# Three edits to an attention-plus-MLP kernel on one Trainium2 core: states of the last output pieces, the rule ahead of each logits step, and the first w1 loads

## The chip, the core and the metric

The kernel runs on one core of a Trainium2 chip. The core has five engines with instruction streams of their own: TensorE (PE, matmuls and their weight loads), VectorE (DVE), ScalarE (ACT), GpSimd (POOL) and SyncE (SP), which here issues all DMAs. They meet at semaphores. Matmul results go to PSUM, which has eight banks of 512 float32 columns on 128 partitions. The metric is the device time of one execution in microseconds, as the median over several executions. Less is better.

## The reference

The inputs are x (2048 tokens by 1024), four 1024 x 1024 weights, a gate per head and an MLP over tokens with hidden size 3584. All are bfloat16. Cut to what matters:

```python
xn = layernorm(x)
# A: 32 heads of 32, 4 segments of 512 tokens, a memory M, z carried from segment to segment
q, k, v = heads(xn @ wq), heads(xn @ wk), heads(xn @ wv)
for s in range(4):
    p     = softmax(qs @ ks.T * scale + causal_mask)
    a_dot = p @ vs
    a_mem = (phi(qs) @ M) / (phi(qs) @ z + 1e-6)
    o_s   = g * a_mem + (1 - g) * a_dot
    M, z  = M + phi(ks).T @ vs, z + sum(phi(ks))
A = concat(o_s) @ wo
# B: token-mixing MLP, over tokens and not over features
h = layernorm(xn)
B = (gelu(h.T @ w1 + b1) @ w2 + b2).T
out = x + A + B
```

So one sum of three parts comes out, and the MLP mixes the 2048 tokens: w1 is 2048 x 3584 and w2 is 3584 x 2048.

## The kernel before

**Framework.** The program is straight-line. A `Res` is the state of a buffer: its last writer and its readers. `FW.op`, `FW.dma` and a matmul group call `_waits`, which makes the engine wait for the writer of what is read and, for what is written, for its writer and its readers:

```python
        for r in writes:
            ...
            for t in r.r.values():
                add(t)
```

A store to DRAM records itself as a reader of the buffer state that it is given. `FW` also keeps a planned clock of each engine (`now`, `clock`, `settle`), on which the order of the attention part is worked out while the program is built. All matmuls are issued in `mm`, so that the profile shows them on line 217; all DMAs are on line 245.

**Start (`loads`, `norm_and_first_hidden`).** x comes in 16 chunks of 128 tokens (256 KB each), and the first 512 columns of w1 in 16 chunks of 128 rows (128 KB each). SyncE issues them in a written-out order: x0, x1, w1 chunk 0, x2, x3, w1 chunks 1 to 3 in one, x4, x5, w1 chunks 4 and 5, and so on. For each chunk c: mean and variance (`stats`, on ScalarE for c in `ACT_STATS`, which has 1, 2, 4, 6 and so on, otherwise on VectorE), the factor 1/sigma (`scale`, GpSimd), the normalised h (`ln_h`, VectorE, line 837), and `early_hidden(c)`, which is eight matmuls of 512 columns on TensorE into all eight banks. VectorE's order is h of x0, h of x1, the statistics of x3, h of x2, half the statistics of x5, h of x3, and so on. Before any data is there, `warm` runs fourteen matmuls on zeros.

**Hidden (`hidden`).** The other 24 blocks of 128 hidden units, two halves each, sixteen matmuls a half, with gelu on ScalarE. TensorE is the bound there.

**Attention and output (`attention_and_out`).** Heads come in units of four; a pass p takes two units. A pass has these TensorE steps in a given list (`crit`): a logits step (`window(p, 0)`), q and k projections, a second logits step, a v projection, four weighing steps (`weigh`: p @ v, for later segments also the memory), a third logits step, q and k, four weighing steps, v. A logits step has ten or twelve matmuls with 32 rows each into six or seven banks at once; ScalarE takes the exponential of each bank (line 1073), which empties it, and GpSimd masks the diagonal blocks (line 1081). A logits step is a `wall`: no later step of the list is taken before it.

Between them go **dense steps** (`_Fill`): the second MLP product, one matmul of 512 columns each. A dense group makes half of one block of 128 output tokens: 28 steps for the 3584 hidden units, and for blocks of the first three segments eight more with wo. It holds one bank from its first step to its last, after which VectorE empties the bank into `stg` (line 1341). `left()` tells the steps that the open group still has:

```python
    def left(self):
        return 0 if self.at == 0 else self.size() - self.at
```

It gives 0 when no group is open. `can(now)` is true when the next dense step has its inputs and, for the first of a group, a free bank by the planned clock. `_Flow.run` picks, at each point of TensorE's planned clock, a step of the list if one is ready (its banks free for 120 ns, `MARGIN`) and the dense work is not behind its goal for this pass (`GOALS`), otherwise a dense step. The rule on line 505 holds back a logits step while an open group has one to five steps left.

**Tail (`tail`).** The last segment's output rows, which hold x and the MLP part already, are loaded back into `fin[0..3]`. For each of the eight pieces (i, h) of 128 rows by 512 columns, `part` adds the wo product in eight matmuls, VectorE adds the bank to `fin` (line 1253), and SyncE stores the piece. The first five pieces are taken in three rounds over the heads, since the last heads come late. The last piece (3, 1) is cut into columns 0 to 256 and 256 to 512, and both halves use the state `R_fin[3][1]`. At the very end SyncE waits for all stores (line 272).

Of the kernel before, what the change touches and what calls it, by code (L numbers as in the profile page):

```python
# [346 lines left out]
def _after(*groups):  # L347

    toks = {}
    for r in groups:  # L350
        for t in list(r.r.values()) + ([r.w] if r.w is not None else []):
            cur = toks.get(t.key)
            if cur is None or cur.val < t.val:
                toks[t.key] = t
    return toks
# [7 lines left out]
class _Flow:  # L363
# [118 lines left out]
    def run(self, goals):  # L482
        fw, fill = self.fw, self.fill
        stall = 0
        for t in self.crit:
            self.in_stage[t.stage] = self.in_stage.get(t.stage, 0) + 1
        self.stage_n = dict(self.in_stage)
        while self.crit:
            now = fw.now["pe"]
            nxt = self.advance(now)  # L490
            pick, soon = None, []
            for t in self.crit[:self.LOOK]:
                if t.left == 0 and len(self.free) >= t.banks:
                    bs = sorted(self.bank_t(b) for b in self.free)[:t.banks]
                    r = max([fw.ready(t.reads, t.writes)] + bs)
                    if r + self.MARGIN <= now:
                        pick = t
                        break
                    soon.append((r, t))
                if t.wall:  # L500
                    break
            stage = self.crit[0].stage
            n_left = self.in_stage[stage]
            ahead = fill.done >= goals[stage] + (goals[stage + 1] - goals[stage]) * (1 - n_left / self.stage_n[stage])
            if pick is not None and (ahead or not fill.can(now)) and not (pick.wall and 0 < fill.left() <= 5
                                                                          and fill.can(now)):
                self.emit_pe(pick)
                continue
            if fill.can(now):
                fill.step()  # L510
                continue
            late = [t for r, t in soon if r <= now]
            if late:
                self.emit_pe(late[0])
                continue
            when = [x for x in [r for r, _ in soon] + [nxt, fill.when()] if x is not None]
            when = [x for x in when if x > now] or [now + 50]
            fw.now["pe"] = min(when)
            stall += min(when) - now
            self.stalls.append((now, min(when) - now, [t.fn.__qualname__ for t in self.crit[:2]], fill.at))  # L520
        self.stall = stall
        return stall
# [21 lines left out]
class _Kernel:  # L544
# [170 lines left out]
    def loads(self):  # L715
        fw = self.fw
        fw.op("pool", lambda e: e.memset(self.mhalf[:], -0.5), writes=[self.R_mhalf])
        fw.op("pool", lambda e: e.memset(self.brow[:], 0.0), writes=[self.R_brow, self.R_brow2])
        fw.op("act", lambda e: e.activation(self.ln_t[:, 0, 0:1], self.mhalf[:, 0:1], ACT.Gelu_apprx_tanh),
              reads=[self.R_mhalf], writes=[self.R_st[0]], ns=1500)  # L720
        self.load_x(0, 1)
        self.load_x(1, 1)
        self.load_w1(0, 1)
        self.load_x(2, 1)
        self.load_x(3, 1)
        self.load_w1(1, 3)
        for c in range(4, 16, 2):
            if c == 4:
                self.load_x(4, 1)
                self.load_x(5, 1)  # L730
            else:
                self.load_x(c, 2)
            self.load_w1(c, 2)
            if c == 6:
                fw.dma(self.brow[0:N_FCH, :], self.B_b1.rearrange("(c q) -> c q", q=P), reads=[self.R_brow],
                       writes=[self.R_brow])
                fw.dma(self.brow[32:32 + N_TCH, :], self.B_b2.rearrange("(c q) -> c q", q=P), reads=[self.R_brow2],
                       writes=[self.R_brow2])
        fw.dma(self.beta_sb[:], self.A_beta.partition_broadcast(P), writes=[self.R_beta])
        self.w1_srcs = [self.B_w1[:, fp * 256:(fp + 1) * 256].rearrange("(c p) f -> p c f", p=P)  # L740
                        for fp in range(N_FCH // 2)]
        fw.dma(self.w1slot[2], self.w1_srcs[2], writes=[self.R_w1s[2]])
        self.w1_next = 3
# [482 lines left out]
    def tail(self):  # L1226
        fw, fl = self.fw, self.flow
        s = N_SEG - 1
        e = _Arena(self.nc, self.early_base, self.early_end)
        wait = _after(*self.R_wv)  # L1230
        fin = [e.take(f"fin{i}", [P, D_MODEL], BF16) for i in range(4)]
        R_fin = [[Res(f"fin{i}_{h}", wait) for h in range(2)] for i in range(4)]
        for i in range(4):
            fw.dma(fin[i][:], self.out_d[:, 4 * s + i, :], reads=[self.R_out[4 * s + i]], writes=R_fin[i],
                   record_reads=False)
        self.fill_left = self.fill.total - self.fill.done
        self.fill.rest()
        fl.advance(10 ** 9)
        order = [(i, h) for i in range(4) for h in range(2)]
        bank = {}  # L1240

        def part(ih, j0, j1, c0=0, c1=512):
            i, h = ih
            if j0 == 0:
                bank[ih, c0] = fl.take_bank()
            b = bank[ih, c0]
            with fw.group(reads=[self.R_wo] + self.R_oT[s % 2][j0:j1], writes=[self.R_bank[b]] if j0 == 0 or j1 == 8 else []):
                for jc in range(j0, j1):
                    fw.mm(self.ps[:, b, c0:c1], self.oT[s % 2][:, jc, i * P:(i + 1) * P],
                          self.wo_sb[:, jc, h * 512 + c0:h * 512 + c1], start=(jc == 0), stop=(jc == 7))  # L1250
            if j1 == 8:
                dst = fin[i][:, h * 512 + c0:h * 512 + c1]
                fw.op("dve", lambda e: e.tensor_tensor(dst, self.ps[:, b, c0:c1], dst, op=ALU.add),  # L1253
                      reads=[self.R_bank[b], R_fin[i][h]], writes=[R_fin[i][h]], ns=170 + (c1 - c0))
                fl.free.append(b)
                fw.dma(self.out_d[:, 4 * s + i, h * 512 + c0:h * 512 + c1], dst, reads=[R_fin[i][h]],
                       writes=[Res("o")], is_output=True)

        for j0, j1 in ((0, 6), (6, 7)):
            for ih in order[:5]:  # L1260
                part(ih, j0, j1)
        for ih in order[:5]:
            part(ih, 7, 8)
        for ih in order[5:7]:
            part(ih, 0, 8)
        part(order[7], 0, 8, 0, 256)
        part(order[7], 0, 8, 256, 512)


class _Fill:  # L1270
# [121 lines left out]
```

## Time and profile before

| what | value |
|---|---|
| median of 6 runs | 696.36 us (696.27 to 696.82) |
| the profiled execution | 696.82 us, of which the span of instructions is 694.8 us |
| TensorE busy | 688.5 us (99%), clock granted 1.000 |
| VectorE, ScalarE, GpSimd busy | 268.1, 282.0, 117.5 us |
| DMA | 77.32 MB, 111 GB/s mean over the span, 319 in the first fortieth |

By stage, with TensorE's busy time in each:

| stretch (us from the start) | what | TensorE busy |
|---|---|---|
| 0 to 9.24 | loads, first normalisations, warm-up, chunk 0 | 7.25 |
| 9.24 to 214.8 | first MLP product, first projections | 205.56 |
| 214.8 to 676.9 | attention passes with dense steps | 461.47 |
| 676.9 to 694.8 | tail | 14.21 |

Times in the trace count from the start of the span. Each instruction has its start, its length and, where its engine sat idle ahead of it, what ended that idle time (`<-`). A matmul of 512 columns is shown with 379 ns, but matmuls overlap: the next one starts 216 ns later. That spacing, and not the length, is what a matmul costs in a row of them.

### The profile page before, as it was taken

What the parts mean: (1) busy time and instruction counts of PE and PEld (TensorE: products, weight loads), DVE (VectorE), ACT (ScalarE), POOL (GpSimd) and SP (SyncE); (2) the same over time, 40 slices, a digit from 0 to 9 for tenths busy, and PEclk for the clock granted to TensorE, in tenths of its full rate; (3) what the DMA queues carried; (4) which work ended last, traced back from release to release, by engine and by line L of the source; (5) the groups of instructions that cost most, each with busy time, mean ns of one, the idle gap of its engine ahead of it and who ended that gap; (6) DMA issues with size and microseconds to landing.
All of it is one profiled execution on the core that took longest, in us unless ns stands there. A gap on an engine that the chain in (4) does not pass through costs nothing.

```text
span 694.8 us, 11585 instructions
## 1 busy us (share of the span) xinstructions
PE 688.5 (99%) x4822; PEld 329.2 (47%) x4822; DVE 268.1 (39%) x602; ACT 282.0 (41%) x513; POOL 117.5 (17%) x235
## 2 busy tenths in 40 slices
PE   8999999999999999999999999999999999999997
PEld 3444444444444544544445454444445444444553
DVE  6731100000002433434555464655546454444544
ACT  7431111122236364454544525454543525444350
POOL 5810000000001121221202212121212212121230
PEclk9999999999999999999999999999999999999999
DMA  9377666223038445446262543527263342524204
GB/s 319 107 182 180 153 169 202 84 60 101 1 122 169 103 94 133 105 105 137 46 153 65 124 102 75 124 52 152 49 150 83 85 109 53 121 62 107 50 18 142
DMA packets 211325, 77.32 MB, mean 111 GB/s; under 512 B 173770, under 2 KB 203594, under 8 KB 211274
## 3 DMA queue, kind: packets, MB, share of 16 engines
q1 hardware_dynamic: 211274, 76.59, 44.2%
q8 instruction: 38, 0.62, 0.4%
q14 instruction: 13, 0.11, 0.0%
HBM read 59.79 MB, written 5.24 MB: 94 GB/s over the span
## 4 chain that ended last, share of the span: by engine, by line
PE 97%; DMA 1%; SPq 0%; DVE 0%; ACT 0%; issue 0%; DVEq 0%
PE ps_all L217 97%; DMA w1all<-in_B_w_dram 1%; SPq L245 0%; DMA out_dram<-fin 0%; DVE fin L1253 0%; DVE stg L1341 0%; ACT etmp L961 0%; ACT vA L977 0%; ACT kT L977 0%; DVE etmp L962 0%; DVEq L65 0%; DVE pkT L964 0%
## 5 line engine op out<-in xcount | busy, mean ns | idle before, releaser
L217 PE MATMUL ps_all<-gT,w2h 128*128 128x512 bf16 x896 | 229.3, 379 | 0.6 <-DVE stg L1341 0.4
L1073 ACT ACTIVATE pT<-ps_all 128x512 bf16<-128x512 f32 x320 | 161.9, 619 | 110.2 <-PE ps_all L217 110.2
L217 PE MATMUL ps_all<-h,w1all 128*128 128x512 bf16 x896 | 193.7, 379 | 0.7 <-DMA w1all<-in_B_w_dram 0.7
L1081 POOL TENSOR_SCALAR_AFFINE_SELECT pT<-pT 128x256 bf16<-128x256 bf16 (+3 forms) x176 | 91.3, 524 | 546.2 <-ACT pT L1073 542.2
L217 PEld LDWEIGHTS ps_all<-h,w1all 128*128 128x128 bf16 x896 | 87.5, 98 | 106.9 <-DMA w1all<-in_B_w_dram 1.2
L217 PEld LDWEIGHTS ps_all<-gT,w2h 128*128 128x128 bf16 x896 | 79.6, 97 | 82.6 <-issue 7.9
L951 ACT ACTIVATE gT<-ps_all,bc 128x512 bf16<-128x512 f32 x56 | 37.7, 689 | 140.4 <-PE ps_all L217 140.4
L1119 DVE CAST ost<-ps_all 128x264 bf16<-128x264 f32 (+1 forms) x128 | 50.5, 396 | 82.0 <-PE ps_all L217 81.4
L217 PEld LDWEIGHTS ps_all<-vA,pT 128*128 128x128 bf16 x1280 | 50.6, 96 | 30.0 <-POOL pT L1081 0.5
L217 PE MATMUL ps_all<-xnT,wq 128*128 128x512 bf16 x256 | 60.5, 379 | 0.0
L217 PE MATMUL ps_all<-xnT,wk 128*128 128x512 bf16 x256 | 60.5, 379 | 0.0
L217 PE MATMUL ps_all<-wv_sb,xnT 128*128 128x512 bf16 x256 | 60.2, 379 | 0.0
L217 PE MATMUL ps_all<-vA,pT 128*128 128x33 bf16 x1280 | 52.0, 178 | 0.0
L978 DVE CAST qT<-ps_all 128x512 bf16<-128x512 f32 x29 | 20.0, 691 | 80.5 <-PE ps_all L217 80.5
L977 ACT ACTIVATE vA<-ps_all 128x512 bf16<-128x512 f32 x18 | 10.8, 598 | 90.6 <-PE ps_all L217 90.6
L889 DVE TENSOR_SCALAR gcol<-gcol 128x32 f32<-128x32 f32 x1 | 0.2, 181 | 118.3 <-ACT gcol L887 118.3
L217 PEld LDWEIGHTS ps_all<-xnT,wk 128*128 128x128 bf16 x256 | 25.1, 98 | 30.2
L217 PEld LDWEIGHTS ps_all<-xnT,wq 128*128 128x128 bf16 x256 | 25.0, 98 | 30.2 <-issue 0.2
L217 PEld LDWEIGHTS ps_all<-wv_sb,xnT 128*128 128x128 bf16 x256 | 25.0, 98 | 30.2 <-ACT pT L1073 0.2
L977 ACT ACTIVATE kT<-ps_all 128x512 bf16<-128x512 f32 x32 | 19.1, 597 | 39.1 <-PE ps_all L217 39.1
L217 PE MATMUL ps_all<-wo_sb,oT 128*128 128x512 bf16 x128 | 34.3, 379 | 0.0
L962 DVE TENSOR_SCALAR etmp<-etmp 128x512 bf16<-128x512 bf16 x48 | 17.6, 366 | 39.8 <-ACT etmp L961 39.7
(68 smaller groups left out, 424.5 us busy)
## 6 DMA issues: line engine op xcount, KB each, us to landing
w2h<-in_B_w_dram SPq DMA_DIRECT2D x64, 224.0 KB, 3.2
w1all<-in_B_w_dram SPq DMA_DIRECT2D x12, 1024.0 KB, 5.3
wq<-in_A_wq_dram SPq DMA_DIRECT2D x32, 256.0 KB, 2.8
wk<-in_A_wk_dram SPq DMA_DIRECT2D x32, 256.0 KB, 2.8
stg<-in_A_x_dram SPq DMA_DIRECT2D x16, 256.0 KB, 3.6
out_dram<-stg SPq DMA_DIRECT2D x16, 256.0 KB, 3.1
xin<-in_A_x_dram SPq DMA_DIRECT2D x5, 512.0 KB, 7.7
wv_sb<-in_A_wv_dram SPq DMA_DIRECT2D x2, 1024.0 KB, 9.2
```

What stands on the lines that cost most here:

```text
L217: ins = self.nc.tensor.matmul(out, *args, **kwargs)
L889: fw.op("dve", lambda e: e.tensor_scalar(self.gcol[:], self.gcol[:], 1.0, None, op0=ALU.add), reads=[self.R_gcol], writes=[self.R_gcol])
L951: fw.op("act", lambda e: e.activation(self.gT[:, fc, half * 512:(half + 1) * 512], self.bank(b), ACT.Gelu_apprx_tanh, bias=self.b1c[:, fc: ...
L962: fl.op({"dve": (lambda e: e.tensor_scalar(et[:], et[:], 1.0, None, op0=ALU.min), 294, 330)}, [R_et], [R_et], prio=2)
L977: self.flow.op({"act": (lambda e, b: e.activation(dst, view(self.bank(b)), ACT.Copy), 635, 560), "dve": (lambda e, b: e.tensor_copy(dst, v ...
L978: "dve": (lambda e, b: e.tensor_copy(dst, view(self.bank(b))), 690, 727)},
L1073: fl.op({"act": (lambda e, b, slot=slot: e.activation(pT[:, slot, :], self.bank(b), ACT.Exp, scale=SCALE), 620, 530)}, [], [R[slot]], box= ...
L1081: fl.op({"pool": (lambda e, ap=ap, pat=pat: e.affine_select(ap, ap, pattern=pat, compare_op=ALU.is_ge, fill=0.0, base=0, channel_multiplie ...
L1119: fl.op({"dve": (lambda e, b: e.tensor_copy(dst, self.ps[:, b, 0:n * VW]), 150 + n * 35, 185 + n * 35)}, [], [self.R_ost[o][qb]], box=box, ...
```

## The change

1. **Final pieces.** There are nine pieces (i, h, c0, c1), each with a state of its own. The last piece of 512 columns is cut into 0 to 320 and 320 to 512. The order of the matmuls by piece is otherwise the same.
2. **The rule ahead of a logits step.** `0 < fill.left() <= 5` becomes `fill.left() <= 5`. With no group open `left()` is 0, so the logits step is now held back then too, and a dense step opens a group first, if `can(now)` is true.
3. **First loads.** w1 chunks 0 and 1 are loaded in one DMA (256 KB) ahead of x2, and chunks 2 and 3 in one (256 KB) behind x3. Before, chunk 0 alone (128 KB) was ahead of x2 and chunks 1 to 3 (384 KB) behind x3.

```diff
-            if pick is not None and (ahead or not fill.can(now)) and not (pick.wall and 0 < fill.left() <= 5
-                                                                          and fill.can(now)):
+            if pick is not None and (ahead or not fill.can(now)) and not (pick.wall and fill.left() <= 5 and fill.can(now)):
                 self.emit_pe(pick)
                 continue
...
         self.load_x(0, 1)
         self.load_x(1, 1)
-        self.load_w1(0, 1)
+        self.load_w1(0, 2)
         self.load_x(2, 1)
         self.load_x(3, 1)
-        self.load_w1(1, 3)
+        self.load_w1(2, 2)
...
-        R_fin = [[Res(f"fin{i}_{h}", wait) for h in range(2)] for i in range(4)]
+        pieces = [(i, h, 0, 512) for i in range(4) for h in range(2)]
+        pieces[-1:] = [(3, 1, 0, 320), (3, 1, 320, 512)]
+        R_fin = {x: Res("fin", wait) for x in pieces}
...
                 fw.op("dve", lambda e: e.tensor_tensor(dst, self.ps[:, b, c0:c1], dst, op=ALU.add),
-                      reads=[self.R_bank[b], R_fin[i][h]], writes=[R_fin[i][h]], ns=170 + (c1 - c0))
+                      reads=[self.R_bank[b], R_fin[x]], writes=[R_fin[x]], ns=170 + (c1 - c0))
                 fl.free.append(b)
-                fw.dma(self.out_d[:, 4 * s + i, h * 512 + c0:h * 512 + c1], dst, reads=[R_fin[i][h]],
+                fw.dma(self.out_d[:, 4 * s + i, h * 512 + c0:h * 512 + c1], dst, reads=[R_fin[x]],
                        writes=[Res("o")], is_output=True)
...
-        for j0, j1 in ((0, 6), (6, 7)):
-            for ih in order[:5]:
-                part(ih, j0, j1)
-        for ih in order[:5]:
-            part(ih, 7, 8)
-        for ih in order[5:7]:
-            part(ih, 0, 8)
-        part(order[7], 0, 8, 0, 256)
-        part(order[7], 0, 8, 256, 512)
+        for j0, j1 in ((0, 6), (6, 7), (7, 8)):
+            for x in pieces[:5]:
+                part(x, j0, j1)
+        for x in pieces[5:]:
+            part(x, 0, 8)
```

## What I predict, before seeing the changed kernel run

> **What bounds the kernel now.** I read the page first: TensorE is busy for 688.5 of 694.8 us (99%), at a granted clock of 1.000. A change of order can then win only what TensorE idles, 6.3 us in all. The next view is the chain of waits, in order of time (start, length, what):
>
> ```profile
> 3.14 6.06 DMA w1all<-in_B_w_dram
> ...
> 9.24 205.66 PE ps_all L217 x952
> ...
> 215.67 88.17 PE ps_all L217 x694
> ...
> 306.89 367.42 PE ps_all L217 x2937
> ...
> 690.72 1.52 DMA out_dram<-fin
> ...
> 692.36 0.42 DVE fin L1253
> ```
>
> The reader is to see that TensorE runs in three long stretches and that the chain leaves it at four places: the load of w1 chunks 1 to 3, one place near 215, one near 306, and a DMA at the end. The view of waits for TensorE alone gives sizes (total us, times, longest):
>
> ```profile
> PE ps_all L217 <- DVE gT L758: 1.3, 1, 1.3
> PE ps_all L217 <- DMA w1all<-in_B_w_dram: 0.7, 1, 0.7
> PE ps_all L217 <- DVE stg L1341: 0.4, 1, 0.4
> PE ps_all L217 <- ACT vA L977: 0.2, 1, 0.2
> ```
>
> Apart from the start, there are three stalls. The change has a part for each of them and one for the end. I take the parts from the end backwards.
>
> **The last pieces.** The order of time on VectorE:
>
> ```profile
> 690.27 0.42 DVE L1253 TENSOR_TENSOR fin<-ps_all,fin 128x256 bf16<-128x256 f32 x1 [0.18 <-PE ps_all L217]
> 692.36 0.42 DVE L1253 TENSOR_TENSOR fin<-ps_all,fin 128x256 bf16<-128x256 f32 x1 [1.67 <-DMA out_dram<-fin]
> ```
>
> Both adds write the same state R_fin[3][1], and the store of the first half is recorded as its reader; so the second add waits for that store to land, though they share no column. The change gives each piece a state, and this wait has no other cause. What is late next? TensorE. Its last matmuls have a spacing of 0.216 us at 512 columns and 0.109 at 256, which is 0.418 ns a column: 0.136 at 320 and 0.082 at 192. The last sixteen start at 689.196; 8 x 0.136 puts the second group at 690.284, and 8 x 0.082 puts its end at 690.94 (before: 690.943, so TensorE gains nothing). An add starts 0.20 us after the end of its group, at both widths (689.196 to 689.397; 690.069 to 690.270). So the 320-column add starts at 690.485, takes 0.49 (between the rows 0.42 for 256 and 0.69 for 512) and is done at 690.975; the 192-column add starts at 690.94 + 0.20 = 691.14, when VectorE is free, and takes 0.36. It ends at 691.50 instead of 692.79. Its store is issued 0.03 later; SyncE issued the one before it by 691.33 (0.33 us an issue), so the queue does not hold it. Sum: 692.79 - 691.50 = **1.29 us**.
>
> [...] The last piece has 192 x 2 = 384 B a row; the halves before had 512 B. The row first: the two 64 KB stores took 1.52 us to land, the 128 KB ones 1.7, so 64 KB more cost 0.2 and nearly all is fixed. By the row the 48 KB store takes 1.52 or up to 0.05 less. [...] No store of under 512 B is in the trace; I take 1.52 and keep 1.15 to 1.35.
>
> **A dense group open at each logits step.** Counting dense matmuls in TensorE's order ahead of each of the 48 logits steps shows where none was open: before the first (none done), and before the one at 305.92 (196 done, seven whole groups of 28). At all others a group is open with 6 to 29 steps left, so the new condition bites twice. TensorE there, with a normal one (222.03) in between:
>
> ```profile
> 214.82 0.61 PE L217 MATMUL ps_all<-qT,kT 32*128 32x512 bf16 x10
> 215.67 1.02 PE L217 MATMUL ps_all<-gT,w2h 128*128 128x512 bf16 x4 [0.24 <-ACT vA L977]
> ...
> 222.03 0.61 PE L217 MATMUL ps_all<-qT,kT 32*128 32x256 bf16 x12
> 222.57 1.25 PE L217 MATMUL ps_all<-gT,w2h 128*128 128x512 bf16 x5
> ...
> 305.92 0.61 PE L217 MATMUL ps_all<-qT,kT 32*128 32x256 bf16 x12
> 306.89 0.60 PE L217 MATMUL ps_all<-gT,w2h 128*128 128x512 bf16 x2 [0.36 <-DVE stg L1341]
> ```
>
> From the start of a logits step to the next dense matmul it is 0.54 us where a group is open, 0.85 at 214.82 and 0.97 at 305.92: the step took seven banks and the eighth was still being emptied. **0.31 + 0.43 = 0.74 us** of stall. After the change a dense step opens a group first, out of one of seven free banks; the logits step then has six and waits for that eighth bank. The planner sees it free some 1.05 us on (235 ns behind the matmuls, 635 + 60 for the copy, 120 of margin), which is five dense steps of 0.216 us, so TensorE stays fed. The logits step and its seven exponentials come about 1 us later. Queued behind it are all later attention steps, since it is a wall: the next q and k projections at the first, a v projection and the weighing at the second. Their cover is dense work: 28 steps are to be had each time. Are the drawn-forward steps paid back? In pass 4 the old rule already drew ten dense steps ahead of the step at 305.92, and two followed it instead of five; ahead of the third logits step the counts of passes 1 to 4 are 32, 92, 151, 211, a rise of 60, 59, 60. The goals pull it level within half a pass. Without that cover each step costs 0.216. Extra matmuls: none. I take 0.74 and keep 0 to 0.74.
>
> **w1's first two chunks as one, ahead of x2.** Same bytes and number of DMAs. TensorE's first eight real matmuls start at 6.61 and could hand over to chunk 1 at 8.33; the load lands at 9.20 and they go at 9.245. Chunk 0 had landed at 5.13; the pair (768 KB in all by then) lands between that and x2's 6.35, near 5.7, ahead of 6.61. Chunk 1 then goes at 8.33 (h of x1 is there at 8.09 and 8.41), which is 0.91 earlier. But behind it waits chunk 2, for h of x2:
>
> ```profile
> 6.51 1.04 ACT L801 ACTIVATE xn_tmp<-xin 128x1024 bf16<-128x1024 bf16 x1
> 9.18 0.56 POOL L829 TENSOR_TENSOR ln_r<-ln_t,mhalf 128x1 f32<-128x1 f32 x1
> 9.90 0.53 DVE L837 TENSOR_SCALAR h<-xin,ln_mv,ln_r 128x1024 bf16<-128x1024 bf16 x1
> ```
>
> ScalarE starts x2's statistics at 6.51, GpSimd finishes at 9.74, VectorE normalises from 9.90 to 10.437, and TensorE follows 0.15 later (6.462 to 6.61 for x0): chunk 2 goes at 10.585 at best. Before it went at 10.983. So 0.40 is the most; the other 0.5 is a stall that moves. And x2 is now 128 KB further back on SyncE's queue. x2 landed at 6.345 (2.19 + 4.2); ScalarE has 0.14 of room (6.51 less 0.02 of start-up), and GpSimd to VectorE, which takes 0.11 to 0.14 elsewhere, leaves 0.04 more. A delay d of x2 gives 0.40 - (d - 0.18). [...] The rows: x2 (896 KB issued in all) landed at 6.345 and x3 (1152 KB) at 7.358, so 1024 KB stands at 6.85: d = 0.51. [...] The small w1 load took 0.88 after x1 (4.25 to 5.13). Gains: 0.21 by the rule, **0.07** by the rows, -0.30 by the small load; I take 0.07, the row at the same place in the queue. x3 moves from 7.36 to about 7.97, still before VectorE's 8.33; x4 and later loads stand behind the same bytes. Chunk 3 would go at 12.6 (h at 11.95 after the delay), chunk 4 at 14.4 (13.93 at worst): no further stall, and from there TensorE had none up to 214.8.
>
> **Sum.** 1.29 + 0.74 + 0.07 = 2.10 us off the profiled execution: 694.8 us of span and 2.0 around it make 696.82, so 694.72. The median of the runs shown is 696.36, 0.46 under the profiled one; none of the parts depends on that difference, so the forecast is 696.36 - 2.10 = **694.3 us**.
>
> **Rivals.**
> - *The front turns against it* (0.12): x2 comes 0.88 later and 0.30 is lost: 1.29 + 0.74 - 0.30 = 1.73, 694.6. For it: the slow first w1 load; against it: the next three landings run faster.
> - *The stall at the logits steps moves* (0.15): weighing steps wait for the later exponentials by as much. For it: 0.19 us at 673.93 is such a wait, for GpSimd's mask. Then 1.36 is left: 695.0.
> - *The front gives all it can* (0.07): 693.95.
> - *The change does not do what it says at the end* (0.03): a new wait takes half of the 1.29; 694.9 to 695.
> - *Slower* (0.05): drawn-forward dense steps are not paid back, so the last pass lacks cover. The place is the stretch of fourteen dense steps ahead of 673.9, where TensorE already waits for GpSimd. The price is 0.216 us a step. Ten unpaid steps (two holds) eat the 2.10; four holds are twenty steps, 4.32 us: 696.36 + 2.2 = 698.6. Against it: the payback above, and only two holds in this order.
>
> My forecast has 0.58. Two medians of this kernel less than 0.2% apart (1.4 us) I count as the same, so "faster" ends at 694.97: forecast, front rival, front gain and under half of the moved stall and the half-lost end give 0.84; "same" 0.11, "slower" 0.05. The range: 693.8 is all of the front plus 0.15, 695.3 takes in the moved stall with part of the front lost.
>
> **What would show it.** The wait of 1.67 on the store of fin gone, and adds of 0.49 and 0.36 at the end; no TensorE wait on ACT vA or DVE stg at the logits steps of passes 1 and 4, with about five dense matmuls ahead of each; the wait on w1 gone, and in its place one of 0.5 to 0.9 us for h ahead of chunk 2. Wrong if TensorE shows new waits on exponentials or masks, above all in the last pass, or if ScalarE starts x2 later than about 7.1.

## The result and the profile after

| | median | runs | profiled execution | its span |
|---|---|---|---|---|
| before | 696.37 us | 40 | 696.82 us | 694.8 us |
| changed | 694.81 us | 20 | 694.54 us | 692.5 us |

The ratio of the changed kernel to the one before is 0.9976, with a 95% interval of 0.9970 to 0.9982. That is 1.56 us less by the medians, 1.25 to 2.09 by the interval. The forecast was 694.3 us in a range of 693.8 to 695.3. A second measurement of the changed kernel gave 694.62 against 696.37 (0.9976, 0.9966 to 0.9985).

The two profiled executions differ by more, 2.28 us. The missing 0.72 is in how they lie to their medians: the one of before is 0.45 above its median, the changed one 0.27 below its own. Why that is so is what the experiments are for. First the chain of waits of the changed kernel, from its tenth piece back (start, length, what):

```profile
1.25 9.43 PE ps_all L217 x30
10.69 0.03 issue
10.72 662.61 PE ps_all L217 x4605
673.33 0.03 issue
673.36 16.78 PE ps_all L217 x123
690.14 0.02 issue
690.16 0.36 DVE fin L1254
```

The chain no longer leaves TensorE at 215 or 306, nor for a DMA at the end. There are only two joints: 10.72, where chunk 2 of the first product starts, and 673.36, the wait for GpSimd's mask that was there before. In the view of waits for TensorE only the start is left. (A gap that the shown 379 ns of a matmul nearly fills is not in this view: chunk 2 starts 0.41 us after the matmul before it, and 0.216 is the normal spacing.)

```profile
PE ps_all L217 <- DVE gT L757: 1.3, 1, 1.3
```

VectorE's last adds, in order of time:

```profile
689.50 0.49 DVE L1254 TENSOR_TENSOR fin<-ps_all,fin 128x320 bf16<-128x320 f32 x1 [0.40 <-PE ps_all L217]
690.16 0.36 DVE L1254 TENSOR_TENSOR fin<-ps_all,fin 128x192 bf16<-128x192 f32 x1 [0.17 <-PE ps_all L217]
```

The add of the last piece now waits for TensorE and not for a store. Both have the lengths that the prediction interpolated, 0.49 and 0.36. The last add ends at 690.52, 2.27 us earlier than before. TensorE at the two logits steps in question:

```profile
214.46 1.24 PE L217 MATMUL ps_all<-gT,w2h 128*128 128x512 bf16 x5
215.64 0.61 PE L217 MATMUL ps_all<-qT,kT 32*128 32x512 bf16 x10
216.18 1.04 PE L217 MATMUL ps_all<-gT,w2h 128*128 128x512 bf16 x4
...
303.11 3.83 PE L217 MATMUL ps_all<-gT,w2h 128*128 128x512 bf16 x17
306.87 0.61 PE L217 MATMUL ps_all<-qT,kT 32*128 32x256 bf16 x12
307.42 1.25 PE L217 MATMUL ps_all<-gT,w2h 128*128 128x512 bf16 x5
```

Five dense steps came ahead of the first logits step (none before), and seventeen ahead of the other (ten before). From each logits step to the next dense matmul it is now 0.54 and 0.55 us (0.85 and 0.97 before).

So the profiled pair splits cleanly, with the start of chunk 2 as the mark of the front: 10.98 to 10.72 is 0.26 us, and the two stalls are 0.73. From the end of the last matmul (its start and its spacing) to the end of the last add it was 1.85 and is 0.56, which is 1.29. The sum is 2.28, against the 2.27 by which the last add ends earlier.

### The profile page after: what moved, and what is told of

It reads as the page before. It is cut to its first block, busy times and chain, and to the rows that moved or that the text cites. A ratio compares the mean times of both kernels' runs of the same rounds, so it can differ in the third digit from the quotient of the medians.

```text
span 692.5 us, 11585 instructions
## 1 busy us (share of the span) xinstructions
PE 688.8 (99%) x4822; PEld 329.5 (48%) x4822; DVE 268.1 (39%) x602; ACT 281.9 (41%) x513; POOL 117.8 (17%) x235
## 4 chain that ended last, share of the span: by engine, by line
PE 99%; DVE 0%; issue 0%
PE ps_all L217 99%; DVE fin L1254 0%; DVE gT L757 0%
```

## The experiments

Each time is set beside runs of the kernel before on the same chip. The interval of a difference is 0.6 to 0.9 us to either side. The pieces alone can be told from zero; the rule alone just reaches zero with its interval; differences of some 0.3 us between two variants can't be told.

| run | what | median | before | difference | ratio, 95% |
|---|---|---|---|---|---|
| e1_tail | pieces alone | 695.05 | 696.45 | -1.40 | 0.9983 (0.9974 to 0.9992) |
| e2_rule | rule alone | 695.64 | 696.45 | -0.81 | 0.9991 (0.9982 to 1.0000) |
| e3_loads | loads alone | 696.60 | 696.45 | +0.15 | 1.0003 (0.9994 to 1.0012) |
| e4_same | no change | 696.50 | 696.45 | +0.05 | 1.0002 (0.9993 to 1.0011) |
| e5_after | all three | 694.62 | 696.37 | -1.75 | 0.9976 (0.9966 to 0.9985) |
| e6_rule_tail | rule and pieces | 694.36 | 696.37 | -2.01 | 0.9972 (0.9962 to 0.9983) |
| e7_h_free | all three, early h of x2 and x3 | 694.15 | 696.37 | -2.22 | 0.9967 (0.9955 to 0.9979) |
| e8_cut256 | all three, equal halves | 694.88 | 696.37 | -1.49 | 0.9978 (0.9969 to 0.9987) |
| e9_w1_four | rule, pieces, four chunks ahead of x2 | 695.69 | 696.46 | -0.77 | 0.9990 (0.9981 to 0.9999) |
| e10_x2_first | rule, pieces, x2 ahead of w1 | 694.31 | 696.46 | -2.15 | 0.9969 (0.9957 to 0.9982) |
| e11_closed | rule turned round | 738.81 | 696.46 | +42.35 | 1.0615 (1.0589 to 1.0642) |
| e12_rule_tail2 | rule and pieces again | 694.33 | 696.46 | -2.13 | 0.9970 (0.9959 to 0.9982) |

### One part at a time

e1 has only the part of the diff in `tail`, e2 only that in `run`, e3 only that in `loads`; e4 is the kernel before.

```diff
 e1
-        R_fin = [[Res(f"fin{i}_{h}", wait) for h in range(2)] for i in range(4)]
+        pieces[-1:] = [(3, 1, 0, 320), (3, 1, 320, 512)]
+        R_fin = {x: Res("fin", wait) for x in pieces}
...
 e2
-            ... and not (pick.wall and 0 < fill.left() <= 5
+            ... and not (pick.wall and fill.left() <= 5
...
 e3
-        self.load_w1(0, 1)
+        self.load_w1(0, 2)
...
-        self.load_w1(1, 3)
+        self.load_w1(2, 2)
```

> Only the final pieces are changed (states of their own, 320 + 192); rule and loads are those of before. The profiled pair of before and after differs by 2.30 us of span, the medians by 1.56: 0.7 us is missing. Theory A (each part is worth what the two profiles show, and the profiled execution of before was a late one because of its first loads): 1.28 us faster, some 695.1. Theory B (the end of the program is worth less outside the profile, since what follows the last store hides part of it): 0.5 to 0.9 us faster.

> Only the rule ahead of a logits step is changed. Theory A: the two stalls of 0.30 and 0.43 us go and nothing comes in their place: 0.73 us faster, some 695.6; dense steps ahead of the two logits steps 5 and 17 as in the changed kernel. Theory C (stalls at banks that the trace of after doesn't show come in other executions): 0 to 0.3 us faster.

> Only the first w1 loads are changed. From profile to profile the front gave 0.27 us (first matmul of chunk 2 at 10.983 and at 10.718, with the first real matmul 0.17 later). Theory A: in the median it gives about nothing or loses up to 0.4 us, because the profiled execution of before had its w1 chunks 1 to 3 land unusually late (9.20) and most executions do not: 696.3 to 696.8. Theory D (the load of three chunks is slow in every execution): 0.3 to 0.4 us faster, 696.0.

> The kernel before once more, for a second profile of it and for what the measurement makes of no change. Time: within 0.1 us of before by every theory. Theory A: in this profile w1 chunks 1 to 3 land before 8.8 us and TensorE's wait on them is under 0.4 us (0.75 in the first profile). Theory D: they land at about 9.2 again and the wait is 0.7 to 0.8 us.

The pieces alone gave 1.40 and the rule alone 0.81, both near the 1.29 and 0.73 of the profiles. Their medians lie above what theories B and C allow, though the intervals reach down to them; the profiles decide it. In the profiles of e1, e3 and e4, which have the old rule, the two stalls are there each time with the same size (0.31 and 0.43 above the normal spacing). In e2 neither is there. From the start of chunk 2 to that of the last matmul it is 679.85 to 679.89 us in the four profiles with the old rule (before, e1, e3, e4) and 679.14 to 679.17 in eight with the new one (the changed kernel, e2, e5, e6, e8, e9, e10, e12). So from chunk 2 on the profiles of one order agree within 0.04 us; what differs from execution to execution lies ahead of it.

The loads gave nothing, and the profile of e4 shows why. This is its view of TensorE's waits (total us, times, longest):

```profile
PE ps_all L217 <- DVE gT L758: 1.3, 1, 1.3
PE ps_all L217 <- DVE stg L1341: 0.4, 1, 0.4
PE ps_all L217 <- DVE h L837: 0.3, 1, 0.3
PE ps_all L217 <- ACT vA L977: 0.2, 1, 0.2
```

The same kernel, but the wait on w1 of 0.7 us that stood in its first profile is not there. In its place is a wait for h. In this execution chunks 1 to 3 landed at 8.43 and not at 9.20; TensorE lost only 0.28 us on them (a spacing of 0.496 in place of 0.216), and chunk 2 then waited for h of x2. The new loads of e3 don't touch that wait, as TensorE's order of time has it:

```profile
6.81 3.40 PE L217 MATMUL ps_all<-h,w1all 128*128 128x512 bf16 x15
10.76 1.46 PE L217 MATMUL ps_all<-h,w1all 128*128 128x512 bf16 x6 [0.55 <-DVE h L837]
```

The first sixteen matmuls run without a break (the first starts at 6.59, just ahead of this window), which is what the part does. Then TensorE waits longer, 0.55 us, for the same h.

### All three, and the front in question

```diff
 e6, e12: the changed kernel with the loads of before
-        self.load_w1(0, 2)
+        self.load_w1(0, 1)
...
-        self.load_w1(2, 2)
+        self.load_w1(1, 3)
```

```diff
 e7: h of x2 and x3 ahead of the statistics of x3, with the mean and factor of x1
         self.early_hidden(0)
+        self.ln_h(2)
+        self.ln_h(3)
         self.stats(3)
...
+        k = 1 if c in (2, 3) else c
-... self.xin[:, c, a:z], self.ln_mv[:, c, 0:1], self.ln_r2[:, c:c + 1], ...
+... self.xin[:, c, a:z], self.ln_mv[:, k, 0:1], self.ln_r2[:, k:k + 1], ...
```

```diff
 e8
-        pieces[-1:] = [(3, 1, 0, 320), (3, 1, 320, 512)]
+        pieces[-1:] = [(3, 1, 0, 256), (3, 1, 256, 512)]
```

> The changed kernel once more, beside its parts. Alone the parts gave -1.40 (pieces), -0.81 (rule) and +0.15 (loads), which is -2.06 in sum; the changed kernel was measured at -1.56. Theory A (the parts add up, the rest is the spread of the first microseconds from run to run): between -1.6 and -2.2 us. Theory E (the parts get in each other's way): -1.5 or less of a gain, with a stall in its profile that no part alone has.

> The changed kernel with the first loads of before (chunk 0 alone ahead of x2). Theory A (the first matmuls of chunk 2 wait for h of x2, so the earlier w1 gains nothing and the later x2 can only cost): the same as the changed kernel or up to 0.4 us faster, chunk 2 at 10.4 to 10.7 in the profile against 10.7 to 10.8. Theory D (the pair of w1 chunks gains 0.3): 0.3 us slower than the changed kernel.

> The changed kernel with h of x2 and x3 made from the mean and factor of x1, right behind h of x1, so that neither waits for its own statistics (these are still worked out, but not used here; the output is that of other statistics in 256 tokens). Theory A: the wait ahead of chunk 2 goes, chunk 2 starts at 10.0 to 10.2 and chunk 3 at 11.8 to 11.9, and the time falls by 0.4 to 0.7 us against the changed kernel unless h of x4 becomes the next gate (then 0.2 to 0.4). Theory F (chunk 2 is held by its w1 load or by TensorE itself): chunk 2 stays at 10.6 to 10.8.

> The changed kernel with the last piece cut at 256 and not at 320: states of their own, but two equal halves. Theory A (the states give the gain, the cut only shortens the last add): the last add takes 0.42 in place of 0.36 and starts at the same distance from the last matmul, 0.07 us slower than the changed kernel, which the medians can't tell; the last store lands in 1.52. Theory G (a row of 384 B is a cost, so the equal cut with 512 B is better): the last store lands 0.05 or more sooner than that of the changed kernel, and the time is not slower.

e5 gave 1.75 and no stall that a part alone lacks: theory A, as far as its interval goes. e6 was 0.26 us faster than e5 on the same chip, and it has the older loads. Alone that difference is inside the noise; the profiles below carry it.

e7 takes the wait for the statistics of x2 and x3 away (it leaves them out of h). Chunk 2 started at 10.09, right behind chunk 1, chunk 3 at 11.82, and the wait came at chunk 4 (14.02), for h of x4. That is 0.3 us ahead of e5 (14.34), and the time was 0.47 below it, somewhat more than theory A gave for this case and within the noise of it. So chunk 2 was held by h and not by w1 or TensorE, and close behind this wait stands the next one, for h of x4.

e8 tests the cut. VectorE at the end:

```profile
689.24 0.42 DVE L1254 TENSOR_TENSOR fin<-ps_all,fin 128x256 bf16<-128x256 f32 x1 [0.18 <-PE ps_all L217]
690.11 0.42 DVE L1254 TENSOR_TENSOR fin<-ps_all,fin 128x256 bf16<-128x256 f32 x1 [0.45 <-PE ps_all L217]
```

With equal halves and states of their own the second add also waits for TensorE alone. It starts 0.31 us after the start of the last matmul and takes 0.42 (0.36 at 192 columns). The unequal cut is worth these 0.07 us in the profile; the medians (0.26 apart) can't tell. Its last store landed 1.52 us after the issue, that of the changed kernel with its 384 B rows 1.49, both times it was profiled. Theory G did not come true for a store of this size.

### Where x2 stands in the queue, and what an open group is worth

The order of the loads behind x0 and x1:

```diff
 e9: rule and pieces, with                  e10: rule and pieces, with
+        self.load_w1(0, 4)                 +        self.load_x(2, 1)
         self.load_x(2, 1)                           self.load_w1(0, 1)
         self.load_x(3, 1)                           self.load_x(3, 1)
                                                     self.load_w1(1, 3)
```

```diff
 e11: before, with
-            ... and not (pick.wall and 0 < fill.left() <= 5
+            ... and not (pick.wall and 0 < fill.left()
                                                                           and fill.can(now)):
```

> Rule and final pieces as in the changed kernel; all of w1 chunks 0 to 3 in one load (512 KB) ahead of x2, twice the step of the change and more. In the nine profiles so far x2 landed at 6.01 to 6.66 with chunk 0 ahead of it and at 6.42 to 6.79 with chunks 0 and 1. Theory A (x2 is what counts, some 0.33 us later for each 128 KB put ahead of it): x2 lands at about 7.3, chunk 2 of the first matmuls starts at 11.1 to 11.4 behind h of x2, and the time is 0.5 to 0.8 us above that of the same kernel with the loads of before. Theory D (early w1 is what counts): chunk 2 no later than 10.7 and no slower.

> Rule and final pieces as in the changed kernel; x2 is loaded ahead of w1 chunk 0, the other way round from the change, with w1 chunks 1 to 3 in one load behind x3. Theory A: x2 lands by 5.7, h of x2 is then held by VectorE's own order (statistics of x3) and not by x2, chunk 2 starts at 10.4 to 10.6 in every profile; chunk 0's load still lands by 6.6; time equal to rule and pieces with the loads of before, or up to 0.2 us below. Theory D: the later w1 holds chunk 0 or chunk 1, 0.3 us or more slower.

> The kernel before with the rule turned round: a logits step is held back as long as any dense group is open, so that none is open at a logits step (as long as dense work is left). Final pieces and loads as before. Theory A (a logits step with no group open costs 0.30 to 0.43 us, since the step takes seven banks and the eighth is being emptied): most of the 48 logits steps show this stall on TensorE, 10 to 20 us slower in all. Theory C (the two stalls were a matter of these two places, ScalarE and VectorE being late there): the stall comes at some steps only, under 6 us slower.

> Rule and final pieces with the loads of before once more, as the kernel to compare the last two with, and for a second value beside 694.36 us. Theory A: 694.2 to 694.6, chunk 2 at 10.4 to 10.7 (later only if w1 chunks 1 to 3 land after 9). Theory D: 694.7 or more.

The profiles of all runs but e7, sorted by what stands ahead of x2. All are us from the start, from the records of the landings and of the instructions. The old order has chunk 0 alone ahead of x2; "pair" means chunks 0 and 1 in one load there. "w1 next" is the load with chunk 1 (old order) or chunk 2 (pair).

| ahead of x2 | run | x2 landed | w1 next landed | h of x2 done | chunk 2 starts |
|---|---|---|---|---|---|
| nothing | e10 | 6.02 | 8.03 | 10.45 | 10.51 |
| chunk 0 | before | 6.34 | 9.20 | 10.44 | 10.98 |
| chunk 0 | e4 | 6.66 | 8.43 | 10.61 | 10.66 |
| chunk 0 | e1 | 6.15 | 8.51 | 10.45 | 10.51 |
| chunk 0 | e2 | 6.13 | 8.22 | 10.37 | 10.43 |
| chunk 0 | e6 | 6.01 | 7.90 | 10.45 | 10.51 |
| chunk 0 | e12 | 6.34 | 7.97 | 10.58 | 10.69 |
| chunk 0 | e11 | 6.41 | 8.07 | 10.52 | 10.57 |
| chunks 0, 1 | changed | 6.51 | 8.01 | 10.57 | 10.72 |
| chunks 0, 1 | e3 | 6.66 | 8.24 | 10.61 | 10.76 |
| chunks 0, 1 | e5 | 6.79 | 8.09 | 10.74 | 10.89 |
| chunks 0, 1 | e8 | 6.42 | 7.80 | 10.37 | 10.67 |
| chunks 0 to 3 | e9 | 7.74 | - | 11.69 | 11.74 |

The first profile of the kernel before is the only row in which w1 decides: h was done 0.54 us earlier than chunk 2 could start. In the six others of its order chunk 2 starts at 10.43 to 10.69, a mean of 10.56. With the pair it starts at 10.67 to 10.89, a mean of 10.76. x2 itself landed at a mean of 6.29 behind one chunk and 6.60 behind two.

But the later x2 is only part of these 0.20 us. Where x2 landed by 6.51, the changed kernel among them, h of x2 starts 1.49 to 1.51 us after the end of h of x1, which is VectorE's own order. Only at 6.66 and later (e3, e4, e5, e9) is it 1.66 us or more. First the changed kernel, then e4:

```profile
10.04 0.53 DVE L836 TENSOR_SCALAR h<-xin,ln_mv,ln_r 128x1024 bf16<-128x1024 bf16 x1
10.06 0.55 DVE L837 TENSOR_SCALAR h<-xin,ln_mv,ln_r 128x1024 bf16<-128x1024 bf16 x1 [0.21 <-POOL ln_r L829]
```

So h of x2 is done only 0.08 us later in the mean (10.50 to 10.57). The other part follows h. Chunk 2 starts 0.15 us after the end of h with the pair (changed, e3, e5) and 0.06 where it shares its load with chunk 1 (e1, e2, e4, e6, e9, e10, e11). With the pair the program makes TensorE wait at chunk 2 for a load of its own besides h. That load had long landed, and no run shows apart that this second wait takes the 0.09; chunk 4 of e7, which also has a load of its own, starts 0.15 after its h as well. In e8 and e12 TensorE itself came late.

e9 makes the price plain. Its waits:

```profile
PE ps_all L217 <- DMA w1all<-in_B_w_dram: 1.3, 1, 1.3
...
PE ps_all L217 <- DVE h L835: 1.1, 1, 1.1
```

Chunk 2 started at 11.74 and the time was 1.36 us above e12. That is twice what was expected, since x2 came at 7.74 and not at 7.3. (The large w1 load itself, which landed at 6.98, held the first real matmul until 7.03. That cost nothing more, as TensorE then waited 1.1 us for h.) The direction is theory A's. e10 shows the other end: h of x2 follows VectorE's own order, chunk 2 starts at 10.51, and the time equals e12's (694.31 and 694.33). x2 landed at 6.02, though, and not by 5.7: no earlier than in e6 (6.01), where a chunk of w1 stood ahead of it. So in these profiles nothing was gained by x2 earlier than about 6.5.

e11 brings the other cost at most logits steps. A typical place of it on TensorE, and one near its end:

```profile
258.53 0.62 PE L217 MATMUL ps_all<-qT,kT 32*128 32x256 bf16 x12
259.53 0.81 PE L217 MATMUL ps_all<-gT,w2h 128*128 128x512 bf16 x3 [0.39 <-DVE stg L1341]
...
715.08 0.30 PE L217 MATMUL ps_all<-vA,pT 128*128 128x33 bf16 x4 [3.27 <-POOL pT L1081]
```

With no group open, 30 of the 48 logits steps have more than 0.1 us of extra time up to the next matmul, 15.4 us in all. In fifteen passes of sixteen the third logits step shows none (0.545 us): it takes six banks and leaves one. That much is what theory A expected. But the total was 42 us. The rest was not taken apart by a run. The trace points to the order that the rule makes: whole groups are drawn forward ahead of each logits step, and the weighing steps then stand without cover, up to 3.3 us at once where the dense work has run out. The granted clock falls there too: 0.50 from 710 to 715 us, and a mean of 0.988 over this execution, where the kernel before had 1.000. So this run supports the mechanism and gives no clean size for it; e2 gives the size.

## Why the prediction came out as it did

**The end: right.** The wait of 1.67 us on the store was a matter of one shared state, and TensorE was next. Forecast 1.29, profile 1.29, alone 1.40 by the median. The 48 KB store landed 1.49 us after its issue; the sum had taken 1.52.

**The logits steps: right.** Forecast 0.74, profile 0.73, alone 0.81. Dense steps covered the delay, and the drawn-forward steps were paid back: ahead of the third logits step of pass 4 there were 215 dense steps (211 before), and ahead of the first one of pass 5 240 in both kernels. One detail was off: seven steps more ahead of the second place and not five. The wait for GpSimd's mask in the last pass stayed at 0.19 us (673.36 less 672.95 less the spacing). Neither the moved stall nor the slower rival came.

**The front: the term that was mis-sized.** The prediction put it at +0.07 us "by the rows". The failed step is its baseline: "Before it went at 10.983". That was read from the one execution in which w1 chunks 1 to 3 landed at 9.20. In the six others they landed at 7.90 to 8.51, and chunk 2 went at a mean of 10.56 behind h of x2. Against the profiled execution the part did gain (0.26). Against the ordinary one it puts x2 0.30 us later and loses some 0.2: 10.56 to 10.76 in the profiles, +0.15 alone, +0.26 from e6 to e5. Each of the two times is within its noise; all three agree in sign, and e9 shows the cost of a later x2 enlarged. The delay d was also mis-sized: 0.51 was taken as half of the step from x2 to x3 in one execution, and 0.30 was measured as a mean. That step was 1.01 us in the first profile, 1.12 and 1.33 in e2 and e1, and 0.63 to 0.65 in the four others of this order, so one row could not give it. No run shows the 0.21 "by the rule" that stands beside the 0.07 among the gains; the profiles showed the loss of some 0.2 in its place.

Two readings of the prediction held: an x2 up to some 0.18 later costs h nothing (it landed 0.16 later in the changed kernel, and h kept VectorE's order), and TensorE follows h by 0.15. But the second holds only where the chunk has a w1 load of its own; in the old order it is 0.06, and part of the loss lies there. Of its signs, the wait of 0.5 to 0.9 us for h ahead of chunk 2 came out at 0.19 in the changed kernel, whose first real matmul started at 7.07 and not at 6.61, and at 0.71 in e3 by the spacing. (Its rival "the front gives all it can" should read 693.93 by its own terms.)

With -0.2 in place of +0.07 the sum is 1.29 + 0.74 - 0.2 = 1.83, between the two measurements of 1.56 and 1.75 and the 2.01 to 2.13 of the kernel without that part. The 0.27 to the first measurement is inside the intervals and stays open: no profile with the pair of loads was taken of an execution slower than its median, so what the slower ones do is not shown. So of the 0.5 us by which the forecast of 694.3 lies under 694.81, half is the front's sign, and the other half is this open part.

**A better version.** Rule and pieces with the loads of before (694.36 and 694.33 in two measurements), or with x2 first (694.31), lie under the changed kernel (694.62 and 694.81) each time. Both are clearly faster than before (0.9969, 0.9957 to 0.9982 for the latter). That they beat the changed kernel by some 0.3 us is likely, but not shown beyond the intervals.

## What to carry to other kernels

When a stall is taken away at the start of a kernel, ask what the next piece of work waits for, and what the moved load now stands ahead of: an earlier operand only moves the wait if another operand of the next step comes later. Here it also gave that step a load of its own to wait for. The first microseconds of one profile are a poor baseline, since landings there differ by more than the gain in question (here one load landed at 7.90 to 9.20, and the gain looked for was 0.40 us at most); take several profiles of the old kernel before costing such an edit. A wait that comes from two disjoint pieces sharing one buffer state was worth 1.29 us here at the end of the program, most of the 1.52 us that the store took to land. A stall that the instruction order fixes came back with the same size in every profile (0.31 and 0.43 us in the four with the old rule).

## What the runs showed of the hardware that was not expected

The same load of 384 KB landed at 9.20 in one execution and at 7.90 to 8.51 in six others, with the same instructions ahead of it. From the end of h to the first matmul on it TensorE took 0.06 us where h was all that it waited for, and 0.15 where the chunk had a w1 load of its own, though the load had landed.

The clock of TensorE was granted at different times in the warm-up: the trace's own record of the granted clock steps up to 1.0 at 3.96 us in e9, at 7.25 in e12 and in between in the others (5.89 in the kernel before, 6.93 in the changed one), with the first warm-up matmul at 1.25 in each. The fourteen warm-up matmuls have a spacing of 0.427 us until then, and 0.216 after. In most profiles one to six of the spacings were short; in four (the changed kernel, e5, e8, e12) none was. There the warm-up ran to its end at the slow spacing, its last matmul started at about 6.78, and the first real one at 7.07 to 7.20 in place of 6.47 to 6.69 (e9 apart, where the load held it). So 7 to 13 of the thirteen spacings were slow, with the same warm-up in each; what sets the number no trace shows. Since chunk 2 waits for h in most profiles, most of the half microsecond is hidden. In e8 and e12 it is not: h was done at 10.37 and 10.58, and chunk 2 followed chunk 1 at the normal spacing, at 10.67 and 10.69.
